# Exponent-minus-one partly on GpSimd, W1 by column quarters, and a new order for five engines

## The chip, the cores and the metric

The kernel runs on one core of a Trainium2 chip. A core has five engines with a queue each: TensorE (PE in the profile; PEld is its loading of weights), VectorE (DVE), ScalarE (ACT), GpSimd (POOL) and SyncE (SP). SyncE issues DMA transfers, GpSimd issues DMA transfers too and also computes on SBUF; TensorE writes to PSUM, and in this kernel only VectorE and ScalarE read PSUM. The engines wait for one another through semaphores. The metric is the device time of one execution, in microseconds; lower is better.

## The reference

Sorted-block attention feeds a Fourier mixing layer and a two-layer feed-forward network. Shapes: 4 batches, 8 heads, 768 positions, head size 64; the model size is 512 and the hidden size 2048.

```python
P = sort_net                                  # 8 x 8 per head
for _ in range(5):
    P = exp(P - max(P)); P /= sum over rows; P /= sum over columns
k_sorted, v_sorted = P mixed over the 8 blocks of k and of v
scores = 0.125 * q_block @ k_sorted_block.T   # 96 x 96, block by block
attn = exp(scores - max); attn /= sum
x = attn @ v_sorted, heads side by side       # 4 x 768 x 512
u = x + real(fft over positions, then over the model dimension)
un = (u - mean) / sqrt(var + 1e-6)
out = u + relu(un @ w_ch1) @ w_ch2
```

## The kernel before

All four batches go through the same stages: `k` and `v` are mixed by the sorting matrix on TensorE (`kqt`, `v_mix`, `v_mix_two`), scores are formed block by block (`scores`), the attention product follows (`av`), then the Fourier sums over positions (`dft1`) and over the model dimension (`dft2`), the normalisation, a transpose, and the two feed-forward products (`ff1`, `ff2`). Batch 0 uses the plain feed-forward product. Batches 1 to 3 use a scheme with seven products in place of eight (`ff1_seven`, `ff2_chunk`), for which VectorE forms sums of quarters of W1 and W2 (`w1_sums`, `w2_sums`).

The exponent step lies in `scores`. For each of 64 pieces (4 batches, 4 pairs of heads, 2 halves of the sequence, 2 heads) ScalarE writes `exp` of a 96 x 384 block of scores from PSUM to the fp32 tile `ex` (line 1270). A second instruction takes one from it and writes it as fp16 into `eb`, in four runs of 96 columns (line 1283 where VectorE does it, line 1285 where ScalarE does it). The attention product of line 1300 reads `eb`.

W1 is 512 x 2048 in HBM. In SBUF it is `w1sb`, 128 partitions with four row groups `c` of 2048 columns. `load_w1` (line 691) loads one row group for all columns, so a feed-forward product, which adds over the four groups (line 1584), needs all four loads. All loads of weights, `q`, `k`, `v` and tables are issued from GpSimd's queue (line 616), as are the indirect and the adding stores (lines 1612 and 1652). Transposing transfers, the rows of `a_rows` and plain stores are issued from SyncE.

What sets the order: every step is an operation with a number, in the order in which the program creates it, with the engines that may do it and their planned costs (`Plan.add`). There are 1614 of them. The table `ORDER` writes out, for each engine, the numbers in the order in which it takes them; an operation that stands in VectorE's list is done by VectorE. `Plan.schedule` replays these lists with planned durations. It does not change the order. It gives buffers (PSUM banks, `ex`, `eb` and others) to the operations in planned time, and it sets how many idle matmuls of line 2010 (`spins`) are put ahead of planned gaps on TensorE. So a change of the planned durations can change buffer numbers and the places of these idle matmuls, and nothing else. An engine never passes a waiting operation in its list.

Neighbouring operations on TensorE may use the whole array or a part of it (64 x 64 or 64 x 128 tiles, in `kq_four`, `q_four`, `scores`, `v_mix_two`); the table `MODE` names these shapes.

The lines that the steps of the change touch:

Of the kernel before, what the change touches and what calls it, by code (L numbers as in the profile page):

```python
# [12 lines left out]
ALU = mybir.AluOpType  # L13
# [17 lines left out]
FETCH = (190, 255, 6.0, 3.5)  # L31
# [36 lines left out]
    ),  # L68
    "ACT": (
# [27 lines left out]
    ),  # L97
    "DVE": (
# [57 lines left out]
TURN = 0.096  # L156
# [125 lines left out]

class Plan:
    HBM = 390.0
    DLAT = 2.2
    XL = 0.07

    def __init__(self):
# [9 lines left out]
    def add(self, costs, fn, r=(), w=(), prio=None, nbytes=0, tag="",  # L298
            after=()):
# [1743 lines left out]
```

## Time and profile before

| | us |
|---|---|
| median of three runs | 257.46 (257.34 to 257.60) |
| the profiled execution's own time | 256.77 |
| its span, from the first to the last instruction | 255.0 |
| TensorE busy in that span | 241.3 |
| VectorE busy | 225.0 |
| ScalarE busy | 178.0 |
| GpSimd busy | 95.3 |

The times in the profile are microseconds from the start of the span. A group row names the line, the engine, the operation, the tile written and the tiles read, the count, and then the busy time of the group, the mean in nanoseconds, and the idle time of the engine just before. A busy TensorE is not a TensorE at its peak: its matmuls overlap, and their ends are modelled, so a short wait between two of them can hide in its busy time.

### The profile page before, as it was taken

To read this page: it belongs to the slowest core of one execution; us is meant where nothing else is said; L and a number is where in the kernel's file an instruction comes from. 1 tells how busy PE (TensorE), PEld (TensorE's weight loads), DVE (VectorE), ACT (ScalarE), POOL (GpSimd) and SP (SyncE) were. 2 spreads that over 40 slices of the span, in tenths; PEclk is the share of its full clock that TensorE was granted. 3 is DMA by queue.
4 is the path that set the end of the run, shared out by engine and by line. 5 is a ranking of instruction groups with operands and counts; after the bars stand their busy time and mean duration, and the time that the engine had idled before them with its cause. 6 is when DMAs were issued, how large, how long until landed. Compare 5 with 4: busy or idle time off the path is not lost.

```text
span 255.0 us, 7508 instructions
## 1 busy us (share of the span) xinstructions
PE 241.3 (95%) x2975; PEld 163.3 (64%) x2975; DVE 225.0 (88%) x576; ACT 178.0 (70%) x418; POOL 95.3 (37%) x128
## 2 busy tenths in 40 slices
PE   4989989999999999999999999999999999999990
PEld 1356865566666566655556667887667887658880
DVE  4789898899999899989999999998999688799870
ACT  2589898999998999999858898244784523664100
POOL 8975522243708950216446000061240007530070
PEclk9999999999999999999999999999999999999999
DMA  6999999999999998482685123652466304880055
GB/s 128 206 213 305 212 212 217 208 218 248 195 117 123 152 154 138 131 150 53 93 179 114 35 75 63 85 88 38 84 75 71 62 4 63 121 107 0 3 108 139
DMA packets 45688, 31.77 MB, mean 125 GB/s; under 512 B 30554, under 2 KB 39528, under 8 KB 45652
## 3 DMA queue, kind: packets, MB, share of 16 engines
q0 software_dynamic: 26544, 23.59, 59.2%
q1 hardware_dynamic: 19110, 7.72, 16.8%
q8 instruction: 23, 0.38, 0.6%
q14 instruction: 11, 0.09, 0.1%
HBM read 29.07 MB, written 11.53 MB: 159 GB/s over the span
## 4 chain that ended last, share of the span: by engine, by line
PE 80%; ACT 10%; DMA 3%; DVE 3%; issue 2%; ACTq 0%; POOLq 0%
PE bank L1764 22%; PE bank L1864 12%; PE bank L1874 9%; PE bank L1668 9%; PE bank L1584 6%; PE bank L1300 4%; DMA hr<-in_v_dram 3%; PE bank L1261 3%; ACT ks L859 2%; PE bank L1465 2%; ACT ex L1270 2%; PE bank L1374 2%; PE bank L1072 1%; PE bank L877 1%; ACT eb L1285 1%
## 5 line engine op out<-in xcount | busy, mean ns | idle before, releaser
L1612 POOL DMA_INDIRECT out_dram<-u,rows x23 | 37.9, 1646 | 109.9 <-DVE u L1892 66.4
L1270 ACT ACTIVATE ex<-bank 96x384 f32<-96x384 f32 x64 | 29.4, 487 | 2.9 <-PE bank L1261 2.5
L1864 PEld LDWEIGHTS <-hr 128*128 128x128 f16 x288 | 28.0, 98 | 5.1 <-DVE hr L1839 0.4
L1764 PE MATMUL bank<-ut,w1sb 128*128 128x384 f16 x144 | 30.9, 326 | 0.0
L859 ACT COPY bank<-bank 128x384 f32<-128x384 f32 (+1 forms) x42 | 18.6, 445 | 13.8 <-DVE hr L1784 4.9
L1764 PEld LDWEIGHTS <-w1sb 128*128 128x128 f16 x192 | 18.6, 98 | 11.1 <-issue 0.2
L1787 ACT ACTIVATE hr<-bank 128x384 f16<-128x384 f32 x41 | 19.1, 492 | 9.2 <-PE bank L1764 8.7
L1584 PE MATMUL bank<-ut,w1sb 128*128 128x384 f16 x128 | 24.5, 326 | 0.0
L1668 PE MATMUL bank<-w2sb,hr 128*128 128x512 f16 x96 | 24.4, 380 | 0.0
L1874 PEld LDWEIGHTS <-vcx 128*128 128x128 f16 x216 | 21.1, 98 | 3.6
L616 POOL DMA_DIRECT2D kq<-in_q_dram x18 | 16.6, 931 | 7.8 <-PE bank L877 3.7
L1764 PEld LDWEIGHTS <-kq 128*128 128x128 f16 x144 | 13.9, 98 | 8.8 <-issue 0.2
L1300 PEld LDWEIGHTS <-eb 97*128 97x128 f16 x416 | 16.3, 98 | 3.8 <-issue 0.2
L1874 PE MATMUL bank<-kq,vcx 128*128 128x256 f16 x144 | 18.5, 273 | 0.0
L1285 ACT ACTIVATE eb<-ex 96x384 f16<-96x384 f32 x37 | 18.3, 521 | 0.1
L1864 PE MATMUL bank<-w2sb,hr 128*128 128x256 f16 x144 | 17.8, 273 | 0.0
L1772 DVE TENSOR_TENSOR hr<-bank,vsf 128x384 f16<-128x384 f32 x32 | 16.8, 550 | 1.2 <-PE bank L1764 1.0
L1300 PE MATMUL bank<-vsf,eb 97*128 97x65 f16 x416 | 17.4, 193 | 0.2
L1317 DVE TENSOR_TENSOR rt<-bank,rz 128x384 f16<-128x384 f32 x32 | 16.9, 545 | 0.3
L859 DVE COPY bank<-bank 128x384 f32<-128x384 f32 (+1 forms) x24 | 12.1, 508 | 5.3 <-PE bank L1874 3.7
L859 ACT CAST vsf<-bank 96x512 f16<-96x512 f32 x25 | 15.7, 676 | 0.5 <-PE bank L976 0.4
L859 ACT CAST ks<-bank 128x384 f16<-128x384 f32 x29 | 15.1, 559 | 0.9 <-PE bank L1195 0.8
(212 smaller groups left out, 587.2 us busy)
## 6 DMA issues: line engine op xcount, KB each, us to landing
w1sb<-in_moe_w_ch_dram POOLq DMA_DIRECT2D x4, 512.0 KB, 18.0
w2sb<-in_moe_w_ch_dram POOLq DMA_DIRECT2D x4, 512.0 KB, 22.2
hr<-in_v_dram POOLq DMA_DIRECT2D x2, 768.0 KB, 9.2
kq<-in_v_dram POOLq DMA_DIRECT2D x2, 768.0 KB, 12.4
kq<-in_k_dram POOLq DMA_DIRECT2D x8, 192.0 KB, 5.5
kq<-in_q_dram POOLq DMA_DIRECT2D x16, 96.0 KB, 7.2
out_dram<-u SPq DMA_DIRECT2D x6, 256.0 KB, 2.2
out_dram<-u POOLq DMA_DIRECT2D x5, 256.0 KB, 4.6
```

The source lines that it names most:

```text
L859: (nc.scalar.copy if e == "ACT" else V.tensor_copy)(dst, src)
L1270: nc.scalar.activation(ex.ap[0:96], pss[h2].ap[0:96, 0:384], AF.Exp, scale=SCALE),
L1285: nc.scalar.activation(ed, src, AF.Identity, bias=-1.0)
L1300: nc.tensor.matmul(po.ap[:, 65 * T:65 * T + 65], eb.ap[:, e0:e0 + 128], vsf[0:97, vi:vi + 65], start=(n == 0), stop=(n == len(WIN[T]) - 1) ...
L1317: P.add({"DVE": (0.465, 0.56)}, lambda _: V.tensor_tensor(rt.ap[:, :, D * h:D * h + D], po3()[:, :, 0:D], rz.ap[:, :, None].broadcast_to([ ...
L1584: nc.tensor.matmul(ps.ap[:, 0:GT], w1sb[:, c, 128 * fc:128 * fc + 128], ut.ap[:, c, :], start=(c == 0), stop=(c == 3))
L1612: return nc.gpsimd.indirect_dma_start(out.rearrange("b s m -> (b s) m"), bass.IndirectOffsetOnAxis(ap=rows[:, i:i + 1], axis=0), t_, None, ...
L1668: nc.tensor.matmul(ps.ap, hr[g][:, fc, 128 * tt:128 * tt + 128], w2sb[:, fc, :], start=(fc == 0), stop=(fc == 15))
L1764: nc.tensor.matmul(ps.ap[:, 0:GT], lhs[:, c, fi], rhs()[:, c, :], start=(start and c == 0), stop=(c == 1), skip_group_check=True)
L1787: nc.scalar.activation(hr[g][:, fc, :], p.ap[:, 0:GT], AF.Relu)
L1864: nc.tensor.matmul(ps.ap[:, 0:256], lhs[:, fc], rhs[:, fc], start=(start and fc == 0), stop=(fc == 7), skip_group_check=True)
L1874: nc.tensor.matmul(ps.ap[:, 0:256], S.ap[:, fc], rhs[:, fc], start=False, stop=(fc == 7), skip_group_check=True)
```

## The change

Three things change in the program, and the order with them.

1. In `scores`, the subtraction of one may be done by GpSimd as well, by the instruction that VectorE uses. In the new lists 28 of the 64 are GpSimd's, 20 ScalarE's and 16 VectorE's, where ScalarE had 37 and VectorE 27. Of the 28, 17 were ScalarE's and 11 VectorE's. Seven belong to batch 0 (131, 136, 138, 147, 163, 170, 181), seven to batch 1 (346, 353, 364, 367, 385, 394, 401), seven to batch 2 (from 595 to 640) and seven to batch 3 (from 686 to 730).
2. `load_w1` loads 512 columns of all four row groups at a time, and a feed-forward product of batch 0 depends on the quarter that holds its columns, not on all four loads.
3. The planned durations are refitted (`FIT`, `TURN`, `FETCH`, `DLAT`, the delays in `load`), and the replay takes into account that the ninth DMA of a queue waits for the first of the eight before it.

The five lists of `ORDER` are new throughout. TensorE's list holds the same operations and the same count of idle matmuls in another order. Beside the exponent steps, some copies change between ScalarE and VectorE (of the `ks` copies 3 to 6 are VectorE's, of the `vsf` copies 7 to 9, of the `seed` copies 24 to 16, and others). GpSimd's list begins so, before and after (an L is a load or an adding or plain store, E an exponent step):

```text
before  L18-L21, memsets, L22-L27, L334, L117-L122, L430, L431, L28-L31 (W1), L432-L435 (W2), L474 ...
after   L18-L21, memsets, L22-L27, E131, L30 (W1), E138, E136, L122, E147, L119, L334, L121, E181,
        L430, E163, E170, L118, L117, L431, L120, L29, L31, L28 (W1), L432, E364, L433, E346, E353,
        E367, L475, L477, L481, L474, L478, L476, L479, L434, L435, E394, E385, E401 ...
```

In it 117, 118, 120 and 121 are halves of batch 1's `k`, 119 and 122 its `q`, 430 and 431 its `v`, 334 the table `perm`, 27 the table `tab`.

```diff
+MOVES = ("load", "out", "acc", "uX", "qX", "arow")
-FETCH = (190, 255, 6.0, 3.5)
+FETCH = (190, 255, 6.4, 4.1)
...
-TURN = 0.096
+TURN = (0.093, 0.195)
+FIT = {("PE", "sc4"): -0.097, ("PE", "kq4"): -0.096, ("PE", "qT4"): -0.095,
...
-    DLAT = 2.2
+    DLAT = 2.0
...
+        lane = {"POOL": [0.0] * 8, "SP": [0.0] * 8}
...
+                if e in lane and o.tag in MOVES:
+                    t = max(t, lane[e][0])
...
-        o.late = 6.0 if after else 0.0
+        o.late = 1.5 if after else 1.1 if nbytes == 526336 else 0.0
...
     def load_w1(c, prio):
-        load(w1sb[:, c, :], w1v[:, c, :], 1048576, [("w1", c)], prio)
+        f = slice(512 * c, 512 * c + 512)
+        load(w1sb[:, :, f], w1v[:, :, f], 1048576, [("w1", c)], prio)
...
-                    if e == "DVE":
-                        V.tensor_scalar(ed, src, -1.0, None, op0=ALU.add)
+                    if e != "ACT":
+                        (V if e == "DVE" else nc.gpsimd).tensor_scalar(
+                            ed, src, -1.0, None, op0=ALU.add)
                     else:
                         nc.scalar.activation(ed, src, AF.Identity,
                                              bias=-1.0)
-                P.add({"DVE": (0.28, 0.36), "ACT": (0.39, 0.49)}, f,
+                P.add({"DVE": (0.28, 0.36), "ACT": (0.39, 0.52),
+                       "POOL": (0.9, 1.1)}, f,
...
             P.add(pe(mm(GT, 4)), f, r=[(ut, tt, 1) for tt in range(3)]
-                  + [("w1", c) for c in range(4)], w=[ps], prio=pr_pe,
-                  tag="ff1")
+                  + [("w1", fc // 4)], w=[ps], prio=pr_pe, tag="ff1")
...
-                (G3, X11, G3, ALU.subtract, w1k, [("w1", 0), ("w1", 1)]),
+                (G3, X11, G3, ALU.subtract, w1k, [("w1", 2), ("w1", 3)]),
```

More of the change, by code (lines that the diff above doesn't have):

```diff
@@ L155 @@
 MODE = {"vmix2": 4, "kq": 1, "qT": 1, "sc": 2, "kq4": 3, "sc4": 3, "qT4": 3}
-TURN = 0.096
+TURN = (0.093, 0.195)
+FIT = {("PE", "sc4"): -0.097, ("PE", "kq4"): -0.096, ("PE", "qT4"): -0.095,
+       ("PE", "vmix2"): -0.127, ("PE", "sc"): -0.097, ("PE", "kq"): -0.093,
+       ("PE", "qT"): -0.06, ("PE", "psx"): 0.03, ("ACT", "ksev"): 0.05,
+       ("ACT", "em1"): 0.024, ("ACT", "vev"): -0.04, ("ACT", "lt"): 0.05,
+       ("ACT", "y"): -0.03, ("ACT", "exp"): -0.012, ("ACT", "ln"): -0.02,
+       ("DVE", "vcp"): -0.11, ("DVE", "seed"): 0.025, ("DVE", "lt"): 0.08,
+       ("DVE", "bdk"): 0.15, ("DVE", "em1"): -0.015, ("DVE", "rr"): 0.04,
+       ("DVE", "rz"): -0.016, ("DVE", "relu"): 0.009, ("DVE", "hs"): 0.006}
 TRIM = {"ff1": 0.003, "ff2": 0.011, "vmix": 0.025, "kq": 0.03, "sc": 0.089,
@@ L307, in add @@
                      + costs["PE"][2:]}
+            costs["PE"] = (costs["PE"][0], costs["PE"][1] - 0.04) + costs[
+                "PE"][2:]
+        costs = {e: (max(c[0] + FIT.get((e, tag), 0.0), 0.0),) + c[1:]
+                 for e, c in costs.items()}
         o.costs, o.fn, o.nbytes, o.tag = costs, fn, nbytes, tag
@@ L434, in schedule @@
                     if MODE.get(o.tag, 0) != mode:
-                        turn = max(0.0, shut + TURN - t)
+                        turn = max(0.0, shut + TURN[mode > 0] - t)
                     mode = MODE.get(o.tag, 0)
@@ L451, in schedule @@
                 o.end = hbm + self.DLAT + o.late
+            if e in lane and o.tag in MOVES:
+                lane[e] = lane[e][1:] + [o.end]
             order.append(o)
```

212 rows, old and new, of the table ORDER are left out of this document.

## The prediction

> **What bounds the kernel now.** I read the page first (engine totals, slices), then busy times by stage, then the chain in order of time.
>
> ```profile
> span 255.0 us, 7508 instructions
> ...
> PE 241.3 (95%) x2975; PEld 163.3 (64%) x2975; DVE 225.0 (88%) x576; ACT 178.0 (70%) x418; POOL 95.3 (37%) x128
> ...
> GB/s 128 206 213 305 212 212 217 208 218 248 195 117 123 152 154 138 131 150 53 93 179 114 35 75 63 85 88 38 84 75 71 62 4 63 121 107 0 3 108 139
> ```
>
> The totals say TensorE. They average over stages with different limits, so here are the stages (length, then busy us and instruction count of PE, PEld, DVE, ACT, POOL, then clock, DMA share, GB/s):
>
> ```profile
> 12.20:53.20 41.00, 37.89 (x718) 25.48 (x720) 36.99 (x103) 37.85 (x87) 18.00 (x26) 1.00 1.17 226
> ```
> ```profile
> 53.50:95.00 41.50, 41.16 (x777) 26.06 (x769) 39.84 (x88) 38.85 (x93) 23.65 (x31) 1.00 1.47 170
> 95.00:130.00 35.00, 35.00 (x515) 20.78 (x514) 33.34 (x80) 32.21 (x79) 12.45 (x12) 1.00 0.66 120
> 130.00:249.00 119.00, 118.97 (x929) 87.51 (x927) 106.69 (x274) 64.12 (x153) 29.99 (x43) 1.00 0.42 70
> ```
>
> And pieces of the chain (start, length, engine, line, instructions merged):
>
> ```profile
> 106.27 0.97 PE bank L1668 x4
> ...
> 107.64 0.86 PE bank L1668 x4
> ...
> 185.07 8.48 PE bank L1764 x52
> ...
> 219.09 11.20 PE bank L1764 x68
> ...
> 249.07 0.42 DVE eb L1892
> ```
>
> Before about 53 us VectorE and ScalarE are both nearly full (36.99 and 37.85 of 41.00) and TensorE waits for one, then the other. After 130 us TensorE alone sets the pace: 8.48 / 52 and 11.20 / 68 are 163 and 165 ns for a matmul of the same 384 columns, over stretches without a hole. A new order can win nothing there. From the last piece at 249.07 to the end at 255.0 is the tail of the last stores; both versions end TensorE's list with the same six operations (1603, 1567, 1605, 1607, 1588, 1610), so I leave the tail as it is. What can change lies before 130 us, most of it before 53.
>
> **The change part by part.**
>
> ```profile
> L1285 ACT ACTIVATE eb<-ex 96x384 f16<-96x384 f32 x37 | 18.3, 521 | 0.1
> L1283 DVE TENSOR_SCALAR eb<-ex 96x384 f16<-96x384 f32 x27 | 9.2, 352 | 1.0 <-ACT ex L1270 0.8
> L859 DVE CAST vsf<-bank 96x512 f16<-96x512 f32 x7 | 4.8, 681 | 0.0
> L859 DVE CAST ks<-bank 128x384 f16<-128x384 f32 x3 | 1.8, 589 | 0.6 <-PE bank L1165 0.6
> L859 DVE COPY qt<-bank 128x768 f16<-128x768 f16 x1 | 0.9, 943 | 0.0
> L859 DVE COPY qt<-bank 128x384 f16<-128x384 f16 x2 | 1.0, 548 | 0.0
> L859 DVE COPY un<-bank 64x128 f32<-64x128 f32 x4 | 1.1, 286 | 0.3 <-ACT un L859 0.3
> L884 DVE TENSOR_REDUCE vsum<-bank 128x64 f32<-128x512 f32 x2 | 1.4, 678 | 0.0
> L701 POOL MEMSET eb<- 96x1672 f16 x4 | 6.2, 1619 | 0.0
> L707 POOL MEMSET vsf<- 96x128 f16 x1 | 0.7, 721 | 0.0
> ```
>
> *GpSimd's exponent-minus-one.* By the lists, 17 leave ScalarE and 11 leave VectorE: 17 x 0.521 = 8.9 us and 11 x 0.352 = 3.9 us of work. The trace has no such instruction on GpSimd. From below: a memset writes an element in 1619 / 1672 = 0.97 ns, so 384 take 0.37 us. From above: the strided memset takes 721 / 128 = 5.6 ns, 2.16 us. The new one writes runs of 96 halves, like the first, and also reads; I take a read and a write at 0.97 ns with 0.12 us to start (the shortest memset of one element, below): 0.87 us.
>
> *The lists ahead of the first ff1.* I take the operations that VectorE must do before the last copy of the transposed `ut`, which releases the first feed-forward matmul. Against the old list there are 8 exponent operations fewer (8 x 0.352), the two `qt` copies fewer (0.943 + 0.548), but 3 `ks` casts more (3 x 0.589), 2 `vsf` casts more (2 x 0.681), one `vsum` reduction (0.678) and three small copies (3 x 0.286); the rest changes places like for like. That is -4.31 + 4.66 = **+0.4 us**. ScalarE's list ahead of that point:
>
> ```profile
> L859 ACT CAST vsf<-bank 96x512 f16<-96x512 f32 x25 | 15.7, 676 | 0.5 <-PE bank L976 0.4
> L859 ACT CAST ks<-bank 128x384 f16<-128x384 f32 x29 | 15.1, 559 | 0.9 <-PE bank L1195 0.8
> L859 ACT COPY qt<-bank 128x384 f16<-128x384 f16 x6 | 2.8, 483 | 0.9 <-PE bank L1139 0.9
> L859 ACT COPY qt<-bank 128x768 f16<-128x768 f16 x3 | 2.4, 802 | 0.0
> ```
>
> It loses those casts (3 x 0.559 + 2 x 0.676), one exponent operation on balance (0.521), and gains three `qt` copies (2 x 0.483 + 0.802): -3.55 + 1.77 = -1.8 us. So VectorE is the limit left in this stage, and it is not relieved: the room that GpSimd gave was filled with ScalarE's casts.
>
> *Idle time recovered.* VectorE idles 41.00 - 36.99 = 4.0 us in that stage. Its longest wait there is for the transform of line 1072, which reads `tab`, and `tab` lands only then:
>
> ```profile
> DVE hi L859 <- PE bank L1072: 1.2, 1, 1.2
> ```
> ```profile
> 25.89 1.08 POOL L616 DMA_DIRECT2D kq<-in_v_dram  x2 [1.62 <-DMA tab<-k_tab]
> ...
> 29.92 1.14 POOL L616 DMA_DIRECT2D w1sb<-in_moe_w_ch_dram  x2 [1.65 <-DMA hr<-in_q_dram]
> ```
>
> That load keeps its place, so 1.2 stays and the ends are 0 and -2.8. I take the row it is nearest to, the 1.8 us by which ScalarE's list shortens: **-1.8**.
>
> *On the way.* Operations 163 and 170 feed the last two attention products of batch 0, so on GpSimd the last of them is longer by 0.87 - 0.521 = **+0.4** (ends -0.2 and +1.6); the earlier seven have other work of ScalarE and VectorE beside them, and cost their own 0.87 each if that cover is gone.
>
> *Changes of array shape.* Counted in TensorE's list, neighbours of another matmul shape (quarter-array against full) fall from 46 to 41 after the first ff1 and rise from 35 to 42 before it. The two pieces of line 1668 above, 0.97 and 0.86 for the same four matmuls, show the price, 0.11. In the dense part -5 x 0.11 = **-0.55**; before it 7 x 0.11 = 0.8 is covered by TensorE's idle 3.1 us of 41.00, and comes on top if it isn't.
>
> *Stage 53 to 95.* TensorE's idle time there is 41.50 - 41.16 = 0.34; eighteen operations fewer on the two helpers can recover at most about that: **-0.3** (end 0).
>
> *GpSimd beside VectorE.* One VectorE instruction of line 1283 that met a descriptor issue of GpSimd's took 0.57 us for 0.35, and line 1776's spread is as wide:
>
> ```profile
> 86.58 1.68 POOL L616 DMA_DIRECT2D kq<-in_q_dram  x2
> ...
> 109.16 0.12 POOL L1611 MEMSET between<- 128x1 f32 x1
> ```
> ```profile
> 87.88 0.57 DVE L1283 TENSOR_SCALAR eb<-ex 96x384 f16<-96x384 f32 x1 [0.84 <-ACT ex L1270]
> ```
> ```profile
> L1776 DVE TENSOR_SCALAR hr<-hr x48: 224/250/572, 139.7 to 235.5; 128x384 f16<-128x384 f16 x48
> ```
>
> So a meeting costs VectorE 0.22 to 0.32 us. Nine of the moved operations stand ahead of the first ff1, where VectorE is the limit. I let four of nine meet one: 4 x 0.22 = **+0.9** (ends 0 and 9 x 0.87 = 7.8, if each holds VectorE for its full length). The Trainium skill, "SBUF — State Buffer", section "Who interferes with whom", states it harder: GpSimd and a VectorE instruction in a two-port mode (or, against a GpSimd read, with two SBUF inputs) exclude one another for a whole instruction. The 0.57 agrees in kind; by that rule the second rival below is what happens.
>
> *W1 by column quarters.* Each load becomes 512 runs of 2 KB, the shape of W2's:
>
> ```profile
> L616 POOL DMA_DIRECT2D w2sb<-in_moe_w_ch_dram x4 | 3.0, 744 | 7.6 <-DMA kq<-in_v_dram 6.1 <-DMA hr<-in_q_dram 1.2 <-DMA hr<-in_k_dram 0.3
> L616 POOL DMA_DIRECT2D w1sb<-in_moe_w_ch_dram x4 | 2.1, 528 | 2.0 <-DMA hr<-in_q_dram 1.6 <-DMA hr<-in_k_dram 0.2
> ```
> ```profile
> w1sb<-in_moe_w_ch_dram POOLq DMA_DIRECT2D x4, 512.0 KB, 18.0
> ...
> kq<-in_v_dram POOLq DMA_DIRECT2D x2, 768.0 KB, 12.4
> ...
> hr<-in_k_dram POOLq DMA_DIRECT2D x4, 192.0 KB, 8.5
> ```
> ```profile
> 53.53 1.47 PE L1584 MATMUL bank<-ut,w1sb 128*128 128x384 f16 x8
> ```
> ```profile
> 34.16 0.49 ACT L1270 ACTIVATE ex<-bank 96x384 f32<-96x384 f32 x1
> ```
>
> 4 x (0.744 - 0.528) = 0.9 us on GpSimd's queue, hidden, since that queue idles. The first ff1 at 53.53 needs one quarter where it needed all of W1; W1's last load, issued at about 30.5 and 18.0 us under way, had landed by then, so I book no gain. But the loads now stand behind exponent operations in GpSimd's list: three W1 quarters come after operation 170, whose input ends at 34.65, and behind three loads of `k` and one of `v` (3 x 192 + 768 KB). With 3 x 512 KB that is 2.88 MB; at the 212 GB/s of that stretch 13.6 us after 35.5, so 49.1, ahead of need. SP's list is permuted too (stores later, transposes of `q` earlier, ahead of them); it only issues, and its waiters had slack, so nothing; a late `qt` would cost its own delay.
>
> *Sum:* 0.4 - 1.8 + 0.4 - 0.55 - 0.3 + 0.9 = -0.95, against the profiled execution's own 256.77 (0.7 under the median of 257.46): 255.8 there, **256.5** on the median's scale. Under 0.2%, 0.5 us, can't be told from no change.
>
> **The rivals.** *VectorE stays the bound (no change).* If only 0.8 of its idle time comes back, the sum is +0.05: 257.5. For it: its list is not shorter. Against: ScalarE's is.
>
> *The engines exclude each other (slower).* If all nine block a VectorE instruction for half their length, 9 x 0.44 = 3.9 in place of 0.9, the sum is +2.05: 259.5. It decides from 1.85 us of blocking, some four meetings of 0.44. For it: the 0.57 and 0.572. Against: most early VectorE work reads PSUM, and rows such as 0.35 us beside GpSimd issues are common.
>
> *The loads come late (slower).* If those 2.88 MB go at 117 GB/s, the slowest slice near, they need 24.6 us, until 60.1; the fifth ff1, which needs the last quarter, would run at about 55, so +5.1 and, with the gains, 261.6. It decides from about 140 GB/s down (landing at 56.1). Against: the slices there read 208 to 248.
>
> **How the numbers follow.** Forecast 0.58, no change 0.14, exclusion 0.20, late loads 0.08. The forecast's own range is 254.6 (all 2.8 us recovered and no meeting: -2.85) to 256.9. The range for 8 in 10 goes from 254.4 to 259.1: it takes in no change and the lower half of exclusion, and leaves out exclusion at its full price and the late loads. Faster 0.58, same 0.14, slower 0.28.
>
> **What would show it.** In the profile after: 28 rows of GpSimd writing `eb` from `ex`, near 0.87 us; VectorE idle between 12 and 53 us down to about 2.2; the first ff1 a microsecond or so earlier; the stretch after 130 us as dense as now. It is wrong if the GpSimd rows pass 1.3 us, if VectorE rows of lines 1283 or 1334 lengthen beside them, or if a TensorE wait of over 1 us is put down to `w1sb` or to GpSimd.

## The result, and the profile after

The changed kernel takes 263.58 us (263.05 to 264.02) where the kernel before took 257.4 us in the same session: a ratio of 1.0243, 95% interval 1.0217 to 1.027. The profiled execution took 263.05 us with a span of 261.3. The forecast was 256.5 us, with a range that ended at 259.1. Every kernel's time below is a median, and every profile shows a single execution; three of these (265.19 us with the stream broken, 264.83 with memsets, 268.96 with rows again) lie above their medians, so from them single rows and places are read, not totals.

The stages first, with the columns of the table shown before (length; busy us and count of TensorE, its weight loads, VectorE, ScalarE and GpSimd; clock, DMA share, GB/s):

```profile
12.20:53.20 41.00, 38.24 (x680) 25.38 (x683) 36.37 (x97) 35.00 (x76) 26.98 (x29) 0.96 1.04 188
53.50:95.00 41.50, 38.30 (x675) 24.20 (x672) 33.03 (x69) 34.20 (x81) 35.66 (x38) 0.96 1.35 181
95.00:130.00 35.00, 34.89 (x581) 21.59 (x578) 34.08 (x82) 29.93 (x73) 23.45 (x25) 1.00 0.80 119
130.00:255.00 125.00, 123.55 (x993) 90.13 (x992) 112.74 (x289) 68.40 (x162) 38.58 (x49) 1.00 0.41 75
```

The stage from 53.5 to 95 us, which had no hole before (41.16 busy of 41.50), now has 3.2 us of idle TensorE, and VectorE is idle there for 8.5 us where it had been for 1.7. Only GpSimd is busier there (35.66 us for 23.65), and part of that is waiting too, as its rows will show. The granted clock falls to 0.96 in the two stages with holes. For whom they wait is in the groups, the waits and one line's instructions:

```profile
L1302 POOL TENSOR_SCALAR eb<-ex 96x384 f16<-96x384 f32 x28 | 48.3, 1783 | 29.3 <-ACT ex L1289 25.9 <-issue 2.8 <-ACT ny L1549 0.6
```
```profile
ACT ex L1289 <- POOL eb L1302: 8.1, 5, 3.5
```
```profile
PE bank L1184 <- ACT ex L1289: 3.0, 2, 2.8
PE bank L1214 <- ACT ex L1289: 2.1, 1, 2.1
PE bank L1321 <- POOL between L1631: 1.5, 1, 1.5
```
```profile
L1302 POOL TENSOR_SCALAR eb<-ex x28: 1157/1266/5763, 19.7 to 139.4; 96x384 f16<-96x384 f32 x28
L1302 DVE TENSOR_SCALAR eb<-ex x16: 308/356/759, 27.3 to 130.5; 96x384 f16<-96x384 f32 x16
```

One exponent step on GpSimd takes 1.157 us at least, 1.78 in the mean and 5.763 at worst (minimum, median and maximum stand behind the count). ScalarE waits 8.1 us for it (the total, the times, the longest), because `ex` has three buffers and GpSimd holds one of them. TensorE in turn waits 5.1 us for ScalarE's next `ex` and 1.5 us for GpSimd itself (`between` is a small memset that follows the exponent step there); the kernel before has no such waits. The chain in order of time shows the three places where this reached TensorE (start, length, what):

```profile
22.03 3.50 POOL eb L1302
...
67.61 5.77 POOL eb L1302
...
79.47 6.22 POOL kq L634 x8
85.69 7.12 DMA kq<-in_k_dram
...
132.37 2.80 POOL eb L1302
```

At the first it is operation 138. At the second 394 takes 5.77 us, and eight loads of `kq` that stand behind it in GpSimd's queue (`k` of batch 2 among them) go out late; but no TensorE wait is put down to them. At the third 730 and 714 follow one another. Behind 138 us little more happens: by the place in TensorE's list its difference to the kernel before goes from 8.0 to 7.6 us, and a short last wait for VectorE brings it to 8.0 again.

Behind the first two holes something else is lost. When TensorE resumes, its clock is granted at half for 3.4 us (start and end, length, TensorE's busy us, clock, DMA share, GB/s):

```profile
26.10:29.50 3.40, 3.40 (x41) 0.50 0.43 39
73.90:77.30 3.40, 3.36 (x42) 0.50 1.21 220
```

TensorE counts as busy there, so this part of the loss is no idle time and no wait. The two ends, before and after:

```profile
249.07 0.42 DVE eb L1892
```
```profile
257.12 0.42 DVE eb L1912
```

VectorE's last addition is 8.0 us later, while the span is only 6.3 us longer: the tail behind it has become shorter. That was no part of the forecast either.

Why does an instruction of 1.16 us take 5.76? These rows are what VectorE does beside operation 394 (the last one merges three, 4.20 us):

```profile
66.14 1.47 DVE L932 TENSOR_TENSOR vcx<-kq,vbn 128x768 f16<-128x768 f16 x1
67.52 0.74 DVE L1114 SCALAR_TENSOR_TENSOR rr<-ex,pack,bank 64x512 f16<-64x512 f16 x1
68.18 4.20 DVE L932 TENSOR_TENSOR vcx<-kq,vbn 128x768 f16<-128x768 f16 x3
```

Those of line 932 follow one another every 1.40 us, undisturbed, one starting some 80 ns before the other ends, and each reads two tiles of SBUF. The last ends at 72.38, and GpSimd's operation ends 0.99 us later: it did its work when that stream was over. So theory A: a GpSimd operation is held up by VectorE's SBUF work. Its rivals: B, the new order itself is worse; C, GpSimd is simply too slow, everywhere; D, the column quarters of W1 cost time.

### The profile page after: what moved, and what is told of

Same layout as the page of the kernel before. It is cut to its first block, busy times and chain, and to the rows that moved or that the text cites. A ratio compares the mean times of both kernels' runs of the same rounds, so it can differ in the third digit from the quotient of the medians.

```text
span 261.3 us, 7517 instructions
## 1 busy us (share of the span) xinstructions
PE 245.6 (94%) x2975; PEld 166.1 (64%) x2975; DVE 225.5 (86%) x570; ACT 172.4 (66%) x396; POOL 137.4 (53%) x156
## 4 chain that ended last, share of the span: by engine, by line
PE 70%; POOL 10%; DMA 6%; ACT 5%; DVE 4%; issue 3%; POOLq 0%; DVEq 0%
PE bank L1784 21%; PE bank L1884 12%; PE bank L1894 8%; POOL eb L1302 6%; PE bank L1605 6%; PE bank L1688 4%; PE bank L1321 3%; DMA hr<-in_v_dram 3%; DMA kq<-in_k_dram 3%; POOL kq L634 3%; PE bank L1486 2%; PE bank L1395 2%; ACT ex L1289 2%; PE bank L1280 2%; POOL out_dram L1632 2%
## 5 line engine op out<-in xcount | busy, mean ns | idle before, releaser
L1632 POOL DMA_INDIRECT out_dram<-u,rows x24 | 35.5, 1479 | 88.5 <-DVE u L1912 40.2
L1302 POOL TENSOR_SCALAR eb<-ex 96x384 f16<-96x384 f32 x28 | 48.3, 1783 | 29.3 <-ACT ex L1289 25.9
L1784 PE MATMUL bank<-ut,w1sb 128*128 128x384 f16 x144 | 31.0, 326 | 0.0
L878 ACT COPY bank<-bank 128x384 f32<-128x384 f32 (+1 forms) x50 | 21.7, 444 | 10.2 <-DVE hr L1804 4.7
L1784 PEld LDWEIGHTS <-w1sb 128*128 128x128 f16 x192 | 18.7, 98 | 11.1
L1605 PE MATMUL bank<-ut,w1sb 128*128 128x384 f16 x128 | 25.3, 332 | 0.0
L1807 ACT ACTIVATE hr<-bank 128x384 f16<-128x384 f32 x35 | 16.7, 493 | 6.3 <-PE bank L1784 5.6
L1605 PEld LDWEIGHTS <-w1sb 128*128 128x128 f16 x128 | 11.2, 98 | 7.3 <-issue 0.8
L1812 ACT COPY vsf<-bank 128x384 f32<-128x384 f32 x16 | 7.6, 481 | 12.3 <-PE bank L1784 12.1
L878 ACT CAST vsf<-bank 96x512 f16<-96x512 f32 x23 | 14.6, 682 | 1.5 <-PE bank L971 0.9
```

Of the source, the lines that this page charges most:

```text
L878: (nc.scalar.copy if e == "ACT" else V.tensor_copy)(dst, src)
L1302: (V if e == "DVE" else nc.gpsimd).tensor_scalar(ed, src, -1.0, None, op0=ALU.add)
L1605: nc.tensor.matmul(ps.ap[:, 0:GT], w1sb[:, c, 128 * fc:128 * fc + 128], ut.ap[:, c, :], start=(c == 0), stop=(c == 3))
L1632: return nc.gpsimd.indirect_dma_start(out.rearrange("b s m -> (b s) m"), bass.IndirectOffsetOnAxis(ap=rows[:, i:i + 1], axis=0), t_, None, ...
L1784: nc.tensor.matmul(ps.ap[:, 0:GT], lhs[:, c, fi], rhs()[:, c, :], start=(start and c == 0), stop=(c == 1), skip_group_check=True)
```

## The experiments

**None on GpSimd.** The 28 operations go back to the engine that had them before, each put into its list behind its exponent; all else is as changed:

```diff
-        "18 19 20 21 5 6 7 1 2 3 4 10 8 22 23 24 25 26 27 131 30 138 136 122 "
+        "18 19 20 21 5 6 7 1 2 3 4 10 8 22 23 24 25 26 27 30 122 119 334 121 "
...
```

> The changed kernel, its new lists and W1's column quarters kept, but its 28 GpSimd exponent-minus-one operations put back on VectorE (11) and ScalarE (17), each on the engine that had it before. Theory A (a GpSimd operation that reads SBUF is held up by VectorE's SBUF work; this costs the 6.1 us): the loss goes with the operations, 256.5 to 258.5 us. Theory B (the new order itself is worse, GpSimd has no part in it): 262 to 264 us, with the holes of TensorE at 26 and 70 to 86 us still there.

The time is 256.12 us, ratio 0.9943 (0.9921 to 0.9964), 0.4 us below the range of A. The whole loss goes with the operations, and B falls. The stages:

```profile
12.20:53.20 41.00, 40.11 (x721) 25.90 (x720) 38.80 (x108) 36.83 (x83) 19.20 (x26) 1.00 1.22 225
53.50:95.00 41.50, 41.13 (x766) 25.91 (x765) 37.47 (x84) 39.37 (x94) 22.12 (x31) 1.00 1.57 173
```

TensorE's idle time in the first stage is 0.9 us (3.1 before the change, 2.8 after it). That is not time won: the replay puts 40 idle matmuls into this kernel, where the two others have 27, and most of the new ones lie in this stage. These are the idle matmuls alone, with none on GpSimd and before the change:

```profile
12.20:53.20 41.00, 6.10 (x20) 1.51 (x18) 1.00 1.22 225
```
```profile
12.20:53.20 41.00, 2.33 (x8) 0.51 (x6) 1.00 1.17 226
```

But for them the list of TensorE is the same as in the changed kernel, so its operations can be compared one by one: the changed kernel is 2.35 us later behind the first place (1.1 of that is left at 57 us), 5.5 behind the second, 7.1 behind the third and to the end. The second place can be split: 3.0 us are lost before TensorE resumes at 73.94 us, and 1.4 more while its clock is at half; with none on GpSimd the clock is 1.00 in both stages. The late loads of `kq` add nothing: the difference is 5.5 us at 75 us and 5.4 at 96. VectorE's last addition stands at 250.04 in the chain, those 7.1 us earlier. So of the 6.3 us of span, 7.1 are the operations on GpSimd, 1.0 is the rest of the new lists (250.04 against 249.07), and 1.8 come off in the tail.

**Five moved off.** The five longest go to ScalarE:

> The changed kernel with five of its 28 GpSimd operations (138, 394, 702, 730, 714, which took 3.5, 5.8, 4.2, 2.6 and 2.8 us) moved to ScalarE; 23 stay. Theory A: most of the loss sits in these five, +5 at 67 to 86 us and +2 at 130 to 138 us, so 256.5 to 259 us. Theory C (every GpSimd operation is too long, 1.16 us at least where 0.87 was reckoned, and the loss is spread): 5 of 28 of 6.1 us come back, 1.1, so about 262.5 us. Theory B: 263 us.

The time is 258.61 us, ratio 1.0031 (0.9991 to 1.007), as A expected. It stays above the 256.12 us of none on GpSimd: TensorE's list ends 2.2 us behind that kernel's, where the changed one ends 7.1 behind. With 394 gone, another operation meets the stream at the same place, and 136 does so near 22 us:

```profile
22.50 3.91 POOL eb L1302
...
67.79 4.22 POOL eb L1302
```

The length belongs to the place, not to the operation.

**Column quarters alone,** in the kernel before:

> The kernel before with one part of the change alone: W1 loaded by column quarters, and the first feed-forward matmuls waiting for one quarter each. Theory A and B: no change, 257.0 to 257.9 us. Theory D (512 runs of 2 KB cost DMA time or GpSimd issue time, and loads land late): slower, 258.5 us or more, with the row of the loads of w1sb longer than 18.0 us from issue to landing and something behind it late.

The time is 255.9 us, ratio 0.9948 (0.9923 to 0.9974): D falls, and so does the "no change" of A and B. TensorE's list runs within 0.2 us of the kernel before up to its end (the last addition is at 249.13 against 249.07); the gain lies behind it, see the closing wait below.

**Sharing, measured by itself:** streams of one kind of VectorE operation beside four GpSimd exponent steps.

> None of the reference's work: only the GpSimd operation (96x384, f32 to f16, minus one), four in a row, alone and then beside a stream of VectorE operations of one kind, each kind by itself; then a memset of the same block in its place. Theory A: about 1.16 us alone; beside VectorE with two SBUF inputs (plain, strided, f32) or copying SBUF to SBUF it stretches to 2 us or more, in a stream without gaps until that stream ends; beside copies or products from PSUM it stays under 1.3 us; VectorE's operations lengthen by less than a third. Theory A2 (each holds the other, whoever comes first, for a whole instruction): both alternate, a GpSimd operation takes at most 1.16 us more than one VectorE operation. Theory C: 1.16 us in all phases.

```profile
L39 POOL TENSOR_SCALAR eb<-ex x40: 1164/1219/2357, 6.0 to 119.3; 96x384 f16<-96x384 f32 x40
```

| VectorE's stream | GpSimd's operation, us | VectorE's own, us |
|---|---|---|
| none; product or copy from PSUM; reduction | 1.16 | unchanged |
| f16 sum of two SBUF tiles | 1.28 to 1.41 | 0.56, in part 0.74 |
| the same, strided as in line 932 | 1.50, the first 2.36 | 1.49 to 1.55 |
| f16 copy or product with a constant | 1.16 to 1.27 | 0.36 to 0.63 |
| strided copy | 1.89, the first 2.12 | 0.83 to 1.02 |
| f32 sum of two SBUF tiles | 1.55 to 1.61 | 0.69, in part 0.87 |

Which streams count is as A says; PSUM sources and reductions don't. But no GpSimd operation was held until the stream ended: here both take turns (A2), and both pay. One thing differed from the kernel: each VectorE operation wrote the same tile as the last, and followed it after a gap of 35 ns.

**Sharing without gaps:** four destination tiles in turn.

```diff
-            V.tensor_copy(c[:, 0:768], a[:, 0:768])
+            V.tensor_copy(cc[turn()][:, 0:768], a[:, 0:768])
...
```

> The same measurement as the one with streams of a single kind, but VectorE writes four buffers in turn, so that no operation waits for the one before and neighbours overlap by some 80 ns as in the kernel (there each operation followed the last after a gap of 35 ns). Theory A3 (GpSimd gets SBUF only in the gaps between VectorE's operations; a stream without gaps holds it off to its end): beside two-input or SBUF-to-SBUF streams the first GpSimd operation takes as long as the rest of the stream (8 strided ones of 1.4 us: over 8 us), beside PSUM sources about 1.2 us as before. Theory A2 (each takes its turn after one operation): at most 2.5 us, as with the gaps.

```profile
L44 POOL TENSOR_SCALAR eb<-ex x40: 1164/1164/9608, 8.4 to 111.8; 96x384 f16<-96x384 f32 x40
```

Beside f16 copies the first GpSimd operation took 9.61 us and beside f32 sums 9.37, to the end of the stream, with VectorE undisturbed at 0.35 and 0.68 us. A memset beside the copies took 6.74 us for 0.41. Beside f16 sums, strided sums and copies, and products with a constant, they took turns as before (1.16 to 2.29 us). So A3 holds for some streams and A2 for others.

**Kind or moment?** The same once more, with GpSimd's first operation coming a little later each time:

> The measurement with overlapped VectorE streams again, for five kinds of operation, each five times with GpSimd's first operation set a little later each time (by a short memset on GpSimd). Theory P (whether a GpSimd operation is held off to the end of the stream or gets its turns depends on the moment at which it comes): every kind shows both, some times near 1.2 to 1.6 us, some of 3 us or more. Theory K (it depends on the kind alone): copies and f32 sums from two SBUF tiles hold it off each time (3.5 us or more), f16 sums and products with a constant never (under 1.7 us).

These are two of the five trials beside the same f16 sums (0.55 us each), GpSimd's rows and VectorE's:

```profile
15.54 5.23 DVE L57 TENSOR_TENSOR vc<-va,vb 128x768 f16<-128x768 f16 x11
```
```profile
15.78 6.01 POOL L54 TENSOR_SCALAR eb<-ex 96x384 f16<-96x384 f32 x1
```
```profile
23.08 0.15 DVE L47 CAST ex<-eb 128x1 f32<-128x1 f16 x1 [2.32 <-POOL eb L54]
...
23.54 2.50 POOL L54 TENSOR_SCALAR eb<-ex 96x384 f16<-96x384 f32 x2
```

Theory P: each of four kinds showed both, held to the end in 9 of 20 trials (5.7 to 6.9 us for the exponent step, 4.5 to 5.0 for a memset) and in turns in 11. The strided sum took turns in all 5, though 394 was held by it in the kernel; so the kind doesn't decide. In all 9 trials of these four kinds in which VectorE had stood idle for over 2 us just before (the 2.32 in the row), it was not held; of the 11 without such a pause, 9 were. But each of these pauses follows a trial that was held, since VectorE waits for its end, so the runs cannot tell the pause from the turn before. What in the moment decides stays open.

**The stream broken.** In the changed kernel VectorE copies one element behind each subtraction of line 932, and has to wait for the subtraction to do so:

```diff
-                      lambda _, dst=dst, src=src, dr=dr: V.tensor_tensor(
+                      lambda _, dst=dst, src=src, dr=dr: (V.tensor_tensor(
                           dst, src, vbn[:, dr, None, None].broadcast_to(
                               [128, 16, 6, 8]), op=ALU.subtract),
+                          V.tensor_copy(tiny, dst[:, 0, 0, 0:1])),
```

> The changed kernel with one copy of a single element more behind each of the eight strided subtractions of line 932 (it reads what the subtraction wrote, so VectorE waits for it and leaves a gap); nothing is taken away, VectorE has eight instructions more. Theory A3: operation 394 on GpSimd, 5.8 us, falls to 3 us or less, the loss of 5 us at 67 to 86 us shrinks by 2 to 4 us, and the whole takes 259.5 to 262 us. Theory A2 or C: 394 stays near 5.8 us and the whole takes 263.5 to 265 us.

The time is 262.2 us, ratio 1.0113 (1.0069 to 1.0157) where the changed kernel stands at 1.0243: eight instructions more, and by the ratios 3.3 us less (0.013 of 257.4). Operation 394:

```profile
68.23 1.37 POOL L1304 TENSOR_SCALAR eb<-ex 96x384 f16<-96x384 f32 x1 [1.06 <-ACT ex L1291]
```

It takes 1.37 us instead of 5.76, beside the same operations with gaps of 34 ns, and the second place costs TensorE 0.5 us where it cost 4.5. Two other rows of this run limit what it says. Operation 138, beside a stream that got no copies, stays at 3.49 us. But 702, whose stream got none either, falls from 4.23 to 1.83 us, so a shifted moment can free an operation too. The run shows that 394 isn't held where the stream has gaps, as no operation was in the measurement with gaps; that the gaps alone did it is likely, but rests on one row.

**Memsets instead.** GpSimd does 4 of the 384 columns and two memsets of the block, in the same place; the rest of the subtraction is left out.

> The changed kernel with each GpSimd exponent-minus-one replaced by a GpSimd operation on 4 of its columns and two memsets of the block (the subtraction is left out; GpSimd is busy as long, about 1.1 us, in the same place of the same list, and waits for the same exponent, but reads almost nothing). Theory A: without reads it is hardly held up; the rows stay under 0.7 us for each memset and the whole takes 256 to 258 us. Theory C (queue and length): 262 to 264 us.

The time is 261.48 us, ratio 1.0102 (1.0063 to 1.014): neither theory's. The reason is in the rows:

```profile
67.62 4.82 POOL L1302 TENSOR_SCALAR eb<-ex 96x4 f16<-96x4 f32 x1 [1.02 <-ACT ex L1289]
72.50 0.41 POOL L1305 MEMSET eb<- 96x384 f16 x1
```

Four columns, an operation of 0.22 us elsewhere in this run, take 4.82 us at 394's place. I had supposed that a small read escapes; it is held off like a large one. The size of the operation is not the cost, and C falls; five of the 28 moved off had already brought back 4.9 of the 7.1 us.

**The kernel before again,** as a control:

> The kernel before once more, unchanged, as a control of what the comparison can tell: ratio 1.000 within 0.2%, and a tail (from the last addition on VectorE to the end of the span) that shows whether the 5.5 us of the profile before or the 4.4 us of the one with column quarters alone is usual. If the tail varies by a microsecond between runs of the same kernel, the 0.5% of the quarters alone is not theirs.

The time is 257.78 us, ratio 0.9981 (0.9953 to 1.001): its tail is as long as in the first profile (below), and a difference of 0.2% is inside what such a comparison shows of itself.

**Rows again,** the changed kernel with W1 by row groups:

> The changed kernel with one part undone: W1 by row groups, first feed-forward matmuls waiting for all of it; 28 operations on GpSimd as in the change. Theory E (the quarters shorten the wait in which GpSimd closes, from its last store's issue to the end of its DRAIN: 5.1 and 5.2 us in two runs of the kernel before, 3.95 us with quarters alone, 3.3 us in the changed kernel): the closing wait is 4.5 to 5.3 us again and the whole takes 264.3 to 265.3 us. Theory F (the 0.5% of the quarters alone was scatter): 263.6 us, closing wait anywhere between 3.3 and 5.2 us. Theory D (quarters cost time in the middle): 262.5 us or less.

The time is 268.07 us, ratio 1.0316 (1.0262 to 1.0371). By the ratio that is 265.5 us on the scale of the result (257.4), just above the range of theory E, and 1.9 us above the changed kernel, with intervals that overlap. In the profiled execution two things come together. TensorE's first feed-forward product waits for W1 again, and in the changed lists W1 comes late (start and length, the load to its landing):

```profile
42.84 15.39 DMA w1sb<-in_moe_w_ch_dram
```

It lands at 58.23; TensorE's list is 4.5 us later there than in the changed kernel, and 4.3 at the end, other holds having shifted in between. And the closing wait is long again. These rows are GpSimd's closing DRAIN, minimum, median and maximum in ns; the maximum is the wait in which its program ends, begun 1.3 to 1.4 us before its last store has been issued. In order: before, before again, rows again; then quarters alone, changed, none on GpSimd:

```profile
L2038 POOLq DRAIN  x3: 46/103/6414, 247.8 to 254.7; - x3
```
```profile
L2038 POOLq DRAIN  x3: 46/103/6544, 248.7 to 255.7; - x3
```
```profile
L2058 POOLq DRAIN  x3: 46/103/6639, 259.8 to 266.9; - x3
```
```profile
L2038 POOLq DRAIN  x3: 46/103/5267, 247.9 to 253.7; - x3
```
```profile
L2058 POOLq DRAIN  x3: 46/102/4714, 255.4 to 261.0; - x3
```
```profile
L2058 POOLq DRAIN  x3: 46/103/5150, 248.3 to 254.1; - x3
```

Rows: 6.4 to 6.6 us; quarters: 4.7 to 5.3, and 4.96 to 5.37 in the four other kernels with quarters. Theory E holds for the wait. It explains the 255.9 of the quarters alone, whose span is 1.0 us shorter than before with TensorE's end unmoved.

**Halves:** W1 by half the rows and half the columns in the kernel before, to see whether the number of runs does it.

> The kernel before with W1 in four loads of half the rows by half the columns: runs of 4 KB, 1024 in all, where it has 512 of 8 KB and the column quarters have 2048 of 2 KB; first feed-forward matmuls wait for all of W1 as before. It asks what shortens GpSimd's closing wait (5.1 and 5.2 us with rows, 3.3 to 4.0 us with quarters). If it falls with the number of runs: 4.6 to 4.9 us and 256.9 to 257.3 us. If quarters are needed for another reason: 5.0 to 5.3 us and 257.4 us; if any other count shifts it as far: 3.3 to 4.0 us and 256 us. TensorE's times up to the last matmul within 0.3 us of the kernel before in every case.

The time is 257.54 us, ratio 1.0011 (0.9985 to 1.0037), and the DRAIN is no shorter:

```profile
L2040 POOLq DRAIN  x3: 46/103/6816, 248.0 to 255.4; - x3
```

1024 runs of 4 KB don't shorten it. Every kernel with the short wait has 2048 runs of 2 KB, but in each of them the first feed-forward products also wait for one load in place of four. No run parts these two, so which of them shortens the wait stays open, and why.

**Ten kept.** Only the operations that were not held up stay on GpSimd:

> The changed kernel with only the ten operations left on GpSimd that took 1.16 to 1.19 us there (147, 181, 163, 364, 623, 621, 635, 626, 640, 628); the other 18 go back to VectorE and ScalarE. If theory A3 holds and these ten meet no unbroken stream in the shifted timeline either: as with none on GpSimd, 255.6 to 256.6 us, since TensorE idles only 0.9 us in its first 41 without them. If they do meet one: one hold-off of 2 to 4 us more, 257.5 to 260 us.

The time is 257.89 us, ratio 0.9978 (0.9953 to 1.0003): no better than none. Operation 147, 1.19 us in the changed kernel, now took 3.26 us at 23.9 us (made up later); another 1.5 us is lost on TensorE between 108 and 117 us, where none of the ten runs, so this run doesn't settle what ten would be worth.

Two versions beat the changed kernel, and by half a percent the kernel before: the kernel before with column quarters alone (255.9), and the changed one with none on GpSimd (256.12). Between them the runs show no difference.

## Why the prediction was wrong

- *GpSimd beside VectorE, +0.9: the step that failed.* It saw that the two meet, and charged VectorE 0.22 us a meeting, from rows in which VectorE was lengthened beside a descriptor issue. It asked nothing of the other side. In the changed kernel VectorE's stream beside 394 ran undisturbed and GpSimd was held: 5 of 28 operations passed even the upper end of 2.16 us (2.6, 2.8, 3.5, 4.2, 5.8). Putting the 28 back takes 7.1 us off the time of VectorE's last addition. The prediction's own sign of being wrong, GpSimd rows over 1.3 us, is there: 1.78 in the mean.
- *The rival "the engines exclude each other"* had the right mechanism, on the wrong engine: 3.9 us of lost VectorE time, 259.5. The price was ScalarE's 8.1 us of waiting for `ex`, then TensorE's waits, then its half clock. By the Trainium skill ("SBUF — State Buffer", section "Who interferes with whom") GpSimd contends with VectorE in two-port modes and, where it reads SBUF, with VectorE instructions that have two SBUF inputs, but not with reductions. The runs agree: 1.16 us beside reductions (and beside PSUM sources), up to 9.61 beside the others. The same section says that a GpSimd instruction which only writes SBUF does not contend with two-input instructions. A memset beside two-input sums was indeed free (0.41 us). By that section the loser is blocked for one whole instruction of the other; the runs show longer holds, through eleven (6.01 us beside sums of 0.55).
- *0.87 us for the operation.* 1.157 at least, inside the bounds; by itself 28 x 0.29 us of an engine that otherwise idled.
- *On the way, +0.4.* Two operations were named, and the earlier seven were taken as covered. Operation 138 was not: 3.5 us in the chain at 22.03.
- *Stage 53 to 95, -0.3.* Its helpers had eighteen operations fewer, and its TensorE idled 2.9 us more (3.2 for 0.3). I had looked at the load on the helpers and not at how long one exponent step can hold a buffer of `ex`: it is the second place, 3.0 us of waiting and 1.4 at half clock. The loads of `kq` behind it in GpSimd's queue (6.22 us of issuing and 7.12 of transfer in the chain) came late without a further loss on TensorE.
- *Idle time recovered, -1.8.* Nothing of it is seen. In the changed kernel TensorE still idles 2.8 us in the first stage, for 3.1 before, and what ScalarE's shorter list would be worth without the holds no run shows. With none on GpSimd its idle time there falls by 2.2 us, but idle matmuls fill 3.8 us more (6.10 for 2.33), and the first feed-forward matmul starts at 53.7 us, against 53.5 before. VectorE's last addition is at 250.04 against 249.07. On its page TensorE is busy for 243.6 us, against 241.3 before; the 13 more idle matmuls are 3.2 us (12.1 for 8.9), more than the whole difference.

```profile
PE 243.6 (96%) x2988; PEld 164.1 (65%) x2988; DVE 225.8 (89%) x581; ACT 177.5 (70%) x413; POOL 91.6 (36%) x128
```

- *Array shapes, -0.55 behind 138 us.* The difference falls by 0.4 there, so sign and size are about right; the last wait for VectorE takes it back before the end.
- *W1 quarters, 0.* Wrong twice. The tail "as it is" became 1.1 us shorter with quarters alone (4.4 us from the end of the last addition to that of the span, for 5.5). And the loads of W1 were issued from 41.3 to 42.8 us, where the working lets the whole series of loads start at 35.5. With row groups in the same lists the last landed at 58.2, not at 49.1. So the rival "the loads come late" was true of W1 in these lists, and the quarters hid it: 4.5 us in that one execution, 1.9 us, tail included, by the ratios of all runs.
- *SP's order, 0.* The runs do not contradict it; none tested it alone.

## What to carry to other kernels

Before an operation goes to GpSimd because that engine idles, look at what VectorE runs at those moments: beside an unbroken stream that reads two SBUF tiles or copies SBUF to SBUF, even four columns can wait until the stream ends, and with them whatever needs their buffer and whatever stands behind in GpSimd's queue. Price both sides of a meeting. A planner that gives such an operation a fixed duration (here 0.9 to 1.1 us) can't see this, and moving the longest ones away can hand the place to the next. And before idle time that a profile no longer shows is called a gain, see whether idle matmuls fill it.

## What the runs showed of the hardware that was not expected

- Whether GpSimd can be held off goes with gaps of tens of nanoseconds: with 35 ns between VectorE's operations nothing took over 2.4 us; with operations that overlap by 80 ns some took up to 9.6, and others took turns. In the held case VectorE keeps its full speed; taking turns, it pays 0.07 to 0.3 us on some of its operations.
- Adding eight one-element copies to VectorE's list made the changed kernel 3.3 us faster.
- After each of two holes of 2 to 3 us TensorE's clock was granted at half for 3.4 us; after the second this cost another 1.4 us, none of it shown as idle. A hole of 1.5 us, the third, was followed by none.
- Loading W1 by column quarters, with products that wait for one quarter, shortens GpSimd's closing DRAIN from 6.4-6.6 us to 4.7-5.4 us, some 200 us after the load; halves with runs of 4 KB don't (6.8).
